# Two pairs of heads transposed as f32 products with the identity, and two constants of the scheduling planner

## The chip, the cores and the metric

One core of a Trainium2 chip. The metric is the device time of one execution in microseconds (us); lower is better. TensorE (PE) multiplies, PEld is its weight load, VectorE (DVE) and ScalarE (ACT) move results out of PSUM, GpSimd (POOL) issues most transfers.

## The reference, cut to what matters

```python
# q, k, v: (8 batches, 12 heads, 448 rows, 64), f32
scores = q @ k.transpose(...) / sqrt(64)
attn   = maximum(scores, 0)**2 / 448
x      = (attn @ v)                       # to (3584 tokens, 768)
xn     = x / rms(x) * rms_g
out    = (silu(xn @ w_gate) * (xn @ w_val)) @ w_out     # d_ff 1536
```

Heads are worked in six pairs per batch. Scores need K and q with the head dimension on the partitions, so both are transposed first. In batch 0 TensorE does that, as soon as they land.

## The kernel before

All instructions are laid down in a fixed order by a planner that runs while the program is built. It keeps an estimated time for each engine and picks the next instruction by it; on the chip each engine then simply follows its list. Where TensorE has nothing to do before the first feed-forward product, the planner inserts **fillers**: products of constants into a spare bank (psB in the profile), which keep the clock up (the run at threshold 400 shows what happens with too few). The parts that the change touches:

```python
GAP = 110.0                # ns: a smaller planned gap gets no filler
SEM, PSUM, HAND, SW = 50.0, 210.0, 200.0, 95.0    # SW: change of array mode
FLOOR = 5850.0, 8500.0, ...    # ns: the earliest planned landing of each early load
F32_T = 0
...
    if self.warm() and (not times or min(times) > t + self.GAP):
        return t, self.filler
...
def filler(self):
    s = max(self.t) + (self.SW if self.mode != "full" else 0.0)
    cost = self.fill() or 96.0           # 128x224, one product
...
# transposes(): one pair, K in 7 pieces and half of q in 2, for 2 heads
ps = bank.take("psT", BF16, [P, 1024])
for nm, j, c, w, o in steps:
    for hh in range(2):
        nc.tensor.transpose(out=ps[...], in_=ld[nm, b][...], identity=ident[:w, :w])
...
pl.task(2, {"dve": dve_cost(width, 0.52), "act": act_cost(width)}, copy, ...)   # to qkT
```

Of the kernel before, what the change touches and what calls it, by code (L numbers as in the profile page):

```python
# [9 lines left out]
BF16 = mybir.dt.bfloat16  # L10
# [4 lines left out]
U = 7  # L15
UH = 4
# [11 lines left out]
def latest(toks, at=0.0):  # L28
    for k in toks:
        if k.t is None:  # L30
            return None
        at = max(at, k.t)
    return at
# [21 lines left out]
class Planner:  # L55
# [2 lines left out]

    SEM, PSUM, HAND, SW = 50.0, 210.0, 200.0, 95.0
    WARM = 6500.0  # L60
    GAP = 110.0
    either = ("square", "squared")
    SLACK = 0.0
    PEN = 200.0
# [197 lines left out]
    def choose(self, t):  # L262
# [21 lines left out]
        for a in self.auxes + self.sneaks:  # L284
            r = a.ready()
            if r is not None:
                times.append(r)
        if self.warm() and (not times or min(times) > t + self.GAP):
            return t, self.filler
# [51 lines left out]
def kernel(  # L341
# [11 lines left out]
    nc = tc.nc  # L353
    P = nc.NUM_PARTITIONS
    B, H, S, D = q.shape
    T, DM = out.shape
    _, F = moe_w_gate.shape
    assert (T, DM) == (B * S, H * D) and 2 * D == P and S % NCH == 0 and B % 2 == 0 and S == U * D
    PC = S // NCH
# [17 lines left out]
    JOIN = 300.0  # L377
    LAG = 2800.0
    LAG0 = 2050.0
    FLOOR = 5850.0, 8500.0, 9350.0, 10450.0, 11150.0, 11850.0, 13150.0, 14900.0  # L380
    floors = []
    LASTW = (384, 192, 192)
    A2, A3, A5 = (384, 384), (256, 256, 256), (512, 256)
# [2 lines left out]
    WO = (A2, A2, A2, A2)  # L386
    ORDER = "w0-2 w2-4 k w4-6 w6-8 w8-10 K w10-12 v"
    FIRST = "k4-8 q8-12 k8-12 v0-4 v4-12 Q"
    F32_T = 0
    AGATE = 6  # L390
    THIRD = 0
    THIRDV = 3
# [24 lines left out]
    pl = Planner(nc, tc, banks, wide, None)  # L417

    def act_cost(n, per=0.8333):
        return 172.0 + per * n  # L420

    def dve_cost(n, per=1.0417):
        return 156.0 + per * n
# [9 lines left out]
    ident = const.tile([P, P], BF16, name="ident", tag="ident")  # L433
# [8 lines left out]
    ld, ldtok, ldhome = {}, {}, {}  # L442
# [3 lines left out]
    def issue(fn, nbytes, run, need=(), rate=None, ahead=8):  # L446
# [8 lines left out]
        def go(e):  # L455
# [4 lines left out]
            lag = LAG0 if dma["t"] < 5000.0 else 1900.0 if dma["t"] < 6500.0 else LAG  # L460
            at = max(dma["t"] + lag, FLOOR[len(floors)] if len(floors) < len(FLOOR) else 0.0)
            floors.append(at)
# [132 lines left out]
    qkT, kTok, qTok = {}, {}, {}  # L595

    def new_qkT(b):
        if b not in qkT:
            qkT[b] = qtpool.tile([P, HP, 2, S], BF16, name="qkT", tag="qkT")
        return qkT[b]  # L600

    def bank_ready():
        f = [x.free for x in banks if x.free is not None]
        return min(f) if f else None

    def wide_ready(n):
        f = sorted(x.free for x in wide if x.free is not None)
        return f[n - 1] if len(f) >= n else None

    def take_bank():  # L610
        return min((x for x in banks if x.free is not None), key=lambda x: x.free)

    def take_wide():
        return min((x for x in wide if x.free is not None), key=lambda x: x.free)

    def free_bank(bank):
        def then(end):
            bank.free = end + 60.0
        return then

    def transposes(b, pairs, c0, c1, with_k, gate=lambda: True):

        done = Tok()
        for j in pairs:
            if with_k:
                kTok[b, j] = done
            for c in range(c0, c1):
                qTok[b, j, c] = done
        toks = [identTok]
        for j in pairs:  # L630
            for nm in ("k", "q") if with_k else ("q",):
                for hh in range(2):
                    lst = ldtok[nm, b][2 * j + hh]
                    if nm == "q" and b == 0:
                        lst = [lst[0]] if c0 == 0 else [lst[-1]]
                    toks += lst
        n = (c1 - c0) * PC
        width = (S if with_k else 0) + n * len(pairs)

        def ready():  # L640
            if not gate():
                return None
            r, f = latest(toks), bank_ready()
            return None if r is None or f is None else max(r, f)

        def run(s):
            bank = take_bank()
            ps = bank.take("psT", BF16, [P, 1024])
            t = new_qkT(b)
            steps = []  # L650
            end = s
            if with_k and b == 0:
                steps += [("k", pairs[0], u, D, u % UH * P + u // UH * D) for u in range(U)]
                end += pl.SW + U * (29.2 - 56.0)
            elif with_k:
                steps += [("k", pairs[0], c, P, c * P) for c in range(UH)]
            at = S if with_k else 0
            for i, j in enumerate(pairs):
                steps += [("q", j, c, PC, at + i * n + (c - c0) * PC) for c in range(c0, c1)]
            for nm, j, c, w, o in steps:  # L660
                for hh in range(2):
                    nc.tensor.transpose(  # L662
                        out=ps[hh * D : (hh + 1) * D, o : o + w],
                        in_=ld[nm, b][:w, 2 * j + hh, c * D : (c + 1) * D],
                        identity=ident[:w, :w],
                    )
            end += 56.0 * len(steps)

            def copy(e):
                if with_k:  # L670
                    dst = t[:, pairs[0]].rearrange("p t s -> p (t s)")[:, c0 * PC : c0 * PC + width]
                    src = ps[:, :width]
                else:
                    dst = t[:, pairs[0] : pairs[-1] + 1, 1, c0 * PC : c1 * PC]
                    src = ps[:, :width].rearrange("p (j s) -> p j s", s=n)
                if e == "dve":
                    copied[b, pairs[-1]] = nc.vector.tensor_copy(out=dst, in_=src)  # L677
                else:
                    copied[b, pairs[-1]] = nc.scalar.copy(out=dst, in_=src)

            pl.task(
                2, {"dve": dve_cost(width, 0.52), "act": act_cost(width)}, copy, [Tok(end + 200.0)],
                done, free_bank(bank),
            )
            return end

        pl.auxes.append(Aux("transposes", "col", ready, run))

    def transposes_f32(j):

        done = [Tok(), Tok()]
        kTok[0, j] = done[0]
        for c in range(2):
            qTok[0, j, c] = done[1]
        toks = [identTok]
        for hh in range(2):
            toks += ldtok["k", 0][2 * j + hh] + ldtok["q", 0][2 * j + hh][:1]

        def ready():
            r, f = latest(toks), wide_ready(1)  # L700
            return None if r is None or f is None else max(r, f)

        def run(s):
            bank = take_wide()
            ps = bank.take("psT")
            t = new_qkT(0)
            parts = (
                ("k", [(u, D, u % UH * P + u // UH * D) for u in range(U)], S),
                ("q", [(c, PC, c * PC) for c in range(2)], 2 * PC),
            )  # L710
            left = [2]

            def over(t):
                left[0] -= 1
                if not left[0]:
                    bank.free = t + 60.0

            for i, (nm, steps, width) in enumerate(parts):
                for c, w, o in steps:
                    for hh in range(2):  # L720
                        nc.tensor.matmul(
                            out=ps[hh * D : (hh + 1) * D, i, o : o + w],
                            lhsT=ld[nm, 0][:w, 2 * j + hh, c * D : (c + 1) * D],
                            rhs=ident[:w, :w],
                            start=True,
                            stop=True,
                        )
                s += 2.0 * sum(w / 2.4 + 2.5 for _, w, _ in steps)

                def copy(e, i=i, width=width):  # L730
                    (nc.vector.tensor_copy if e == "dve" else nc.scalar.copy)(
                        out=t[:, j, i, :width], in_=ps[:, i, :width]
                    )

                pl.task(
                    2, {"dve": dve_cost(width), "act": act_cost(width)}, copy,
                    [Tok(s + 200.0)], done[i], over,
                )
            return s + pl.SW

        pl.auxes.append(Aux("transposes", "col", ready, run))

    def transposes_wide(b, ja, gate):
# [666 lines left out]
    identTok = pl.task(-1, {"pool": 550.0}, make_ident)  # L1410
# [27 lines left out]
        return sub.total - sum(1 for u in pl.units if u.sub is sub)  # L1438

    for j in range(HP):  # L1440
        if j < F32_T:
            transposes_f32(j)
        else:
            transposes(0, [j], 0, 2, True)
    pl.task(0, {"sp": 500.0}, load_g, [kTok[0, HP - 1]])
    for j in range(0, HP, 3):
        transposes(0, [j, j + 1, j + 2], 2, 4, False, gate=lambda: begun(a0) >= AGATE)
    for j in range(0, HP, 1 + WIDE_T):
        def gate(j=j):
            return getattr(a1, "visited", 0) >= GATE if j < 2 else begun(subs[2]) >= 3 * j - LEAD  # L1450
# [136 lines left out]
```

## Time and profile before

| | before |
|---|---|
| median of the six runs beside the changed kernel | 436.48 us (436.30 to 436.73) |
| span of the profiled run | 434.8 us |
| TensorE busy | 429.8 us |
| fillers | 78, of which 27 before the first transpose |
| first transpose | 6.39 us |
| first feed-forward product (psg) | 25.23 us |

Read it thus: from 25.23 us to the end TensorE has a dense list of feed-forward products, so its end should move with that first psg, and what the change gains or loses should show as a shift of psg. I therefore measure each run by two distances, **from the first transpose to psg** and from psg to the end of the span.

### The profile page before, as it was taken

What the parts mean: (1) busy time and instruction counts of PE and PEld (TensorE: products, weight loads), DVE (VectorE), ACT (ScalarE), POOL (GpSimd) and SP (SyncE); (2) the same over time, 40 slices, a digit from 0 to 9 for tenths busy, and PEclk for the clock granted to TensorE, in tenths of its full rate; (3) what the DMA queues carried; (4) which work ended last, traced back from release to release, by engine and by line L of the source; (5) the groups of instructions that cost most, each with busy time, mean ns of one, the idle gap of its engine ahead of it and who ended that gap; (6) DMA issues with size and microseconds to landing.
All of it is one profiled execution on the core that took longest, in us unless ns stands there. A gap on an engine that the chain in (4) does not pass through costs nothing.

```text
span 434.8 us, 12552 instructions
## 1 busy us (share of the span) xinstructions
PE 429.8 (99%) x5576; PEld 314.9 (72%) x5576; DVE 265.1 (61%) x437; ACT 251.5 (58%) x356; POOL 78.5 (18%) x97
## 2 busy tenths in 40 slices
PE   8999999999999999999999999999999999999996
PEld 6678788964579755885579855795569955699996
DVE  3898984478754676657854578567754577442200
ACT  4878873576663675757743676576744567342222
POOL 8444411062160070006200340001000000000000
PEclk9999999999999999999999999999999999999998
DMA  9999999699799599179917991166103200020023
GB/s 151 193 196 196 203 192 120 132 173 123 106 157 205 110 138 64 38 136 107 124 38 155 152 161 9 37 115 99 28 17 95 74 2 2 2 74 2 2 74 109
DMA packets 134805, 44.68 MB, mean 103 GB/s; under 512 B 104096, under 2 KB 131296, under 8 KB 134752
## 3 DMA queue, kind: packets, MB, share of 16 engines
q0 software_dynamic: 94448, 24.16, 57.7%
q1 hardware_dynamic: 39808, 19.50, 22.2%
q8 instruction: 43, 0.70, 0.7%
q10 hardware_dynamic: 496, 0.24, 0.2%
q14 instruction: 10, 0.08, 0.1%
HBM read 48.76 MB, written 11.01 MB: 137 GB/s over the span
## 4 chain that ended last, share of the span: by engine, by line
PE 98%; DMA 1%; issue 0%; DVE 0%; ACT 0%; POOLq 0%
PE psO L147 26%; PE psv L147 26%; PE psg L147 26%; PE psAV L1024 9%; PE psS L917 7%; PE psT L662 2%; PE psB L1532 1%; DMA k<-in_k_dram 1%; PE psR L938 1%; PE psSS L1206 0%; PE psSS L1130 0%; DVE qkT L677 0%; ACT ost L1336 0%; POOLq L1571 0%
## 5 line engine op out<-in xcount | busy, mean ns | idle before, releaser
L147 PE MATMUL psv<-xn,wv_sb 64*128 64x448 bf16 (+1 forms) x1296 | 170.4, 329 | 0.0
L147 PE MATMUL psg<-xn,wg_sb 64*128 64x448 bf16 (+1 forms) x1296 | 170.0, 329 | 0.0
L860 ACT ACTIVATE r<-psS 128x896 bf16<-128x896 f32 x133 | 119.1, 919 | 33.4 <-PE psS L917 32.6
L147 PE MATMUL psO<-wo_sb,hT 64*128 64x384 bf16 (+2 forms) x1464 | 132.3, 310 | 0.0
L147 PEld LDWEIGHTS <-hT 64*128 64x128 bf16 x1464 | 109.8, 94 | 14.6 <-issue 2.5
L147 PEld LDWEIGHTS <-wg_sb 64*128 64x128 bf16 x1296 | 94.9, 94 | 30.5 <-issue 3.2
L147 PEld LDWEIGHTS <-wv_sb 64*128 64x128 bf16 x1296 | 93.9, 94 | 31.4 <-issue 2.5
L866 DVE TENSOR_TENSOR r<-r 128x896 bf16<-128x896 bf16 (+1 forms) x171 | 99.9, 610 | 12.1 <-ACT r L860 11.4
L1258 DVE TENSOR_TENSOR hT<-sil,psv 128x448 bf16<-128x448 bf16 x96 | 59.2, 617 | 61.4 <-PE psv L147 61.1
L1242 ACT ACTIVATE sil<-psg 128x448 bf16<-128x448 f32 x96 | 52.3, 545 | 47.8 <-PE psg L147 47.6
L917 PE MATMUL psS<-qkT 64*128 64x448 bf16 (+1 forms) x324 | 53.0, 329 | 0.1
L1336 ACT COPY ost<-psO 128x384 f32<-128x384 f32 (+2 forms) x51 | 23.1, 453 | 50.1 <-PE psO L147 49.9
L508 POOL DMA_DIRECT2D vb<-in_v_dram x18 | 13.2, 743 | 180.8 <-PE psg L147 75.2
L1024 PE MATMUL psAV<-r,vb 64*64 64x448 bf16 (+1 forms) x756 | 43.1, 335 | 0.4
L860 ACT ACTIVATE r<-psR 128x896 bf16<-128x896 f32 (+1 forms) x24 | 20.2, 840 | 28.7 <-PE psR L938 28.7
L1055 DVE TENSOR_SCALAR xT<-psAV 128x896 bf16<-128x896 f32 (+1 forms) x20 | 20.4, 1022 | 25.8 <-PE psAV L1024 25.7
L1180 DVE SCALAR_TENSOR_TENSOR xn<-xT,g_sb,rstd 128x448 bf16<-128x448 bf16 (+1 forms) x54 | 30.2, 626 | 7.8 <-ACT rstd L1164 7.7
L555 POOL DMA_DIRECT2D kb<-in_k_dram x42 | 31.6, 795 | 13.1 <-DMA vb<-in_v_dram 5.4
L1024 PEld LDWEIGHTS <-vb 64*64 64x64 bf16 x756 | 18.5, 105 | 20.6 <-PE psAV L1024 8.5
L917 PEld LDWEIGHTS <-qkT 64*128 64x128 bf16 x324 | 19.2, 94 | 9.8 <-issue 1.1
L858 DVE TENSOR_SCALAR r<-psS 128x896 bf16<-128x896 f32 x11 | 12.0, 1087 | 17.6 <-PE psS L917 17.4
L1080 DVE TENSOR_TENSOR x2f<-xT 128x896 f32<-128x896 bf16 x19 | 20.6, 1084 | 2.0 <-ACT xT L1053 2.0
(49 smaller groups left out, 175.2 us busy)
## 6 DMA issues: line engine op xcount, KB each, us to landing
vb<-in_v_dram POOLq DMA_DIRECT2D x14, 384.0 KB, 6.5
kb<-in_k_dram POOLq DMA_DIRECT2D x42, 96.0 KB, 7.6
qb<-in_q_dram POOLq DMA_DIRECT2D x6, 672.0 KB, 10.3
out_dram<-ost SPq DMA_DIRECT2D x7, 336.0 KB, 2.8
wg_sb<-in_moe_w_gate_dram POOLq DMA_DIRECT2D x6, 384.0 KB, 13.1
wv_sb<-in_moe_w_val_dram POOLq DMA_DIRECT2D x6, 384.0 KB, 13.2
wo_sb<-in_moe_w_out_dram POOLq DMA_DIRECT2D x2, 1152.0 KB, 18.8
out_dram<-ost SPq DMA_DIRECT2D x8, 288.0 KB, 2.8
```

The source lines that it names most:

```text
L147: mm = self.nc.tensor.matmul(out=seg.bank["tile"][:, off : off + seg.w], lhsT=lhsT[prt], rhs=rhs[prt], start=(seg.first and h == 0 and i = ...
L555: lambda o=o, i=i: nc.gpsimd.dma_start(out=o, in_=i),
L860: nc.scalar.activation(out=r[:, :, :w], in_=ps[:, :, :w], func=ACT.Relu)
L866: nc.vector.tensor_tensor(out=r[:, :, :w], in0=r[:, :, :w], in1=r[:, :, :w], op=ALU.mult)
L917: nc.tensor.matmul(out=ps[:, hh, o : o + n], lhsT=t[prt, j, 0, c * P : (c + 1) * P], rhs=t[prt, j, 1, sub.q0 : sub.q0 + n], start=True, st ...
L1024: mm = nc.tensor.matmul(out=ps[hh * D : (hh + 1) * D, jj, :n], lhsT=vt[prt, 2 * (ja + jj) + hh, u * D : (u + 1) * D], rhs=r[prt, hh, o : o ...
L1055: nc.vector.tensor_scalar_mul(out=xT[at], in0=ps[:, :, :n], scalar1=inv_attn)
L1080: nc.vector.tensor_tensor(out=got["x2"][:], in0=xT[at], in1=xT[at], op=ALU.mult)
L1180: nc.vector.scalar_tensor_tensor(out=xn[:, kt, q0 : q0 + n], in0=xTs[b, 0][:, kt, q0 : q0 + n], scalar=g_sb[:, kt : kt + 1], in1=rstd[:, q ...
L1242: nc.scalar.activation(out=s[:, :m], in_=ps[:, :m], func=ACT.Silu)
L1258: nc.vector.tensor_tensor(out=h[:, fbs[0] : fbs[-1] + 1, o : o + n], in0=s[:, :m].rearrange("p (f s) -> p f s", s=n), in1=ps[:, :m].rearra ...
L1336: nc.scalar.copy(out=ost[:, c0 : c0 + w], in_=ps[:, :w])
```

## The change

Its intent: transpose the first two pairs with real products, K and q side by side across the border of two f32 banks, so that one instruction copies both; and tune the filler threshold and the first landing to that.

```diff
-    GAP = 110.0
+    GAP = 160.0
-    FLOOR = 5850.0, 8500.0, ...
+    FLOOR = 6000.0, 8500.0, ...
-    F32_T = 0
+    F32_T = 2
...
-            bank = take_bank()
-            ps = bank.take("psT", BF16, [P, 1024])
+            if f32:
+                bank = take_wide()
+                ps = bank.take("psT")[:].rearrange("p a b -> p (a b)")[:, 512 - S :]
+            else:
+                bank = take_bank()
+                ps = bank.take("psT", BF16, [P, 1024])
...
+                    if f32:
+                        nc.tensor.matmul(out=to, lhsT=rows, rhs=ident[:w, :w], start=True, stop=True)
+                    else:
+                        nc.tensor.transpose(out=to, in_=rows, identity=ident[:w, :w])
...
-                2, {"dve": dve_cost(width, 0.52), "act": act_cost(width)}, copy, ...
+                2, {"dve": dve_cost(width, 1.0417 if f32 else 0.52), "act": act_cost(width)}, copy, ...
... (an unused older variant, transposes_f32, is removed)
-            transposes(0, [j], 0, 2, True)
+            transposes(0, [j], 0, 2, True, f32=j < F32_T)
```

More of the change, by code (lines that the diff above doesn't have):

```diff
@@ L379 @@
     LAG0 = 2050.0
-    FLOOR = 5850.0, 8500.0, 9350.0, 10450.0, 11150.0, 11850.0, 13150.0, 14900.0
+    FLOOR = 6000.0, 8500.0, 9350.0, 10450.0, 11150.0, 11850.0, 13150.0, 14900.0
     floors = []
@@ L619, in free_bank, with transposes @@
         return then
-    def transposes(b, pairs, c0, c1, with_k, gate=lambda: True):
+    def transposes(b, pairs, c0, c1, with_k, gate=lambda: True, f32=False):
         done = Tok()
@@ L642, in ready @@
                 return None
-            r, f = latest(toks), bank_ready()
+            r, f = latest(toks), wide_ready(1) if f32 else bank_ready()
             return None if r is None or f is None else max(r, f)
         def run(s):
-            bank = take_bank()
-            ps = bank.take("psT", BF16, [P, 1024])
+            if f32:
[4 more added lines that the diff above has]
+                ps = bank.take("psT", BF16, [P, 1024])
             t = new_qkT(b)
@@ L661, in run @@
                 for hh in range(2):
-                    nc.tensor.transpose(
-                        out=ps[hh * D : (hh + 1) * D, o : o + w],
-                        in_=ld[nm, b][:w, 2 * j + hh, c * D : (c + 1) * D],
-                        identity=ident[:w, :w],
-                    )
+                    to = ps[hh * D : (hh + 1) * D, o : o + w]
+                    rows = ld[nm, b][:w, 2 * j + hh, c * D : (c + 1) * D]
+                    if f32:
+                        nc.tensor.matmul(out=to, lhsT=rows, rhs=ident[:w, :w], start=True, stop=True)
+                    else:
+                        nc.tensor.transpose(out=to, in_=rows, identity=ident[:w, :w])
             end += 56.0 * len(steps)
@@ L681, in run @@
             pl.task(
-                2, {"dve": dve_cost(width, 0.52), "act": act_cost(width)}, copy, [Tok(end + 200.0)],
+                2, {"dve": dve_cost(width, 1.0417 if f32 else 0.52), "act": act_cost(width)}, copy, [Tok(end + 200.0)],
                 done, free_bank(bank),
@@ L685, in run @@
             return end
-        pl.auxes.append(Aux("transposes", "col", ready, run))
-    def transposes_f32(j):
-        done = [Tok(), Tok()]
-        kTok[0, j] = done[0]
-        for c in range(2):
-            qTok[0, j, c] = done[1]
-        toks = [identTok]
-        for hh in range(2):
-            toks += ldtok["k", 0][2 * j + hh] + ldtok["q", 0][2 * j + hh][:1]
-        def ready():
-            r, f = latest(toks), wide_ready(1)
-            return None if r is None or f is None else max(r, f)
-        def run(s):
-            bank = take_wide()
-            ps = bank.take("psT")
-            t = new_qkT(0)
-            parts = (
-                ("k", [(u, D, u % UH * P + u // UH * D) for u in range(U)], S),
-                ("q", [(c, PC, c * PC) for c in range(2)], 2 * PC),
-            )
-            left = [2]
-            def over(t):
-                left[0] -= 1
-                if not left[0]:
-                    bank.free = t + 60.0
-            for i, (nm, steps, width) in enumerate(parts):
-                for c, w, o in steps:
-                    for hh in range(2):
-                        nc.tensor.matmul(
-                            out=ps[hh * D : (hh + 1) * D, i, o : o + w],
-                            lhsT=ld[nm, 0][:w, 2 * j + hh, c * D : (c + 1) * D],
-                            rhs=ident[:w, :w],
-                            start=True,
-                            stop=True,
-                        )
-                s += 2.0 * sum(w / 2.4 + 2.5 for _, w, _ in steps)
-                def copy(e, i=i, width=width):
-                    (nc.vector.tensor_copy if e == "dve" else nc.scalar.copy)(
-                        out=t[:, j, i, :width], in_=ps[:, i, :width]
-                    )
-                pl.task(
-                    2, {"dve": dve_cost(width), "act": act_cost(width)}, copy,
-                    [Tok(s + 200.0)], done[i], over,
-                )
-            return s + pl.SW
         pl.auxes.append(Aux("transposes", "col", ready, run))
@@ L1440 @@
     for j in range(HP):
-        if j < F32_T:
-            transposes_f32(j)
-        else:
-            transposes(0, [j], 0, 2, True)
+        transposes(0, [j], 0, 2, True, f32=j < F32_T)
     pl.task(0, {"sp": 500.0}, load_g, [kTok[0, HP - 1]])
```

## The prediction

> **What bounds the kernel now.** I read the page first, then twenty-microsecond stretches of each engine, then the order in time and the chain of waits of the first 26 us, then the groups of those 26 us by shape.
>
> The page says that one engine sets the time. These are its busy times and the lines of the chain that ended last:
>
> ```profile
> PE 429.8 (99%) x5576; PEld 314.9 (72%) x5576; DVE 265.1 (61%) x437; ACT 251.5 (58%) x356; POOL 78.5 (18%) x97
> ...
> PE psO L147 26%; PE psv L147 26%; PE psg L147 26%; PE psAV L1024 9%; PE psS L917 7%; PE psT L662 2%; PE psB L1532 1%; DMA k<-in_k_dram 1%; PE psR L938 1%; PE psSS L1206 0%; PE psSS L1130 0%; DVE qkT L677 0%; ACT ost L1336 0%; POOLq L1571 0%
> ```
>
> TensorE is the bound, and the feed-forward products alone are 78% of the chain. The stretches show where its few idle microseconds lie (columns: stretch, length, then busy time and count of PE, PEld, DVE, ACT, POOL, then clock and DMA):
>
> ```profile
> 0.00:20.00 20.00, 18.57 (x316) 12.75 (x316) 11.66 (x25) 12.57 (x17) 13.67 (x24) 1.00 1.27 170
> 20.00:40.00 20.00, 20.00 (x365) 15.32 (x360) 16.96 (x33) 15.22 (x22) 9.05 (x12) 1.00 1.46 197
> ```
>
> 1.43 us are idle in the first 20; after that 0.26 us in four dips until 420 us, and 3.3 us in the tail. But busy is not useful: the first 26 us hold 78 matmuls on psB, 12.1 us, whose result nobody reads. They keep the clock up while attention of batch 0 waits for data and for the copies. The first feed-forward matmul starts at 25.23 us, and behind it TensorE never stops. So whatever moves that first psg moves the end by the same amount, and the change, which touches only the start of batch 0, can be worth no more than it gains or loses before 25.23 us.
>
> The order in time around the changed transposes (start, length, engine, line, what; the idle time before and its releaser in brackets):
>
> ```profile
> 6.39 0.41 PE L662 MATMUL psT<-ident,k 64*64 64x64 bf16 x14 [0.41 <-DMA k<-in_k_dram]
> 6.73 0.14 PEld L662 LDWEIGHTS <-qb 112*64 112x64 bf16 x4
> 6.73 0.29 PE L662 MATMUL psT<-ident,qb 112*64 112x112 bf16 x4
> ...
> 7.06 0.51 DVE L677 COPY qkT<-psT 128x672 bf16<-128x672 bf16 x1 [5.54 <-PE psT L662]
> ...
> 7.50 0.11 PEld L1532 LDWEIGHTS <-const-bfloat16-1.0 128*128 128x128 bf16 x2
> 7.51 0.37 PE L1532 MATMUL psB<-const-bfloat16-1.0 128*128 128x224 bf16 x2
> 7.62 0.72 ACT L679 COPY qkT<-psT 128x672 bf16<-128x672 bf16 x1 [3.52 <-PE psT L662]
> 7.80 0.11 PEld L917 LDWEIGHTS <-qkT 64*128 64x128 bf16 x4 [0.19 <-DVE qkT L677]
> ```
>
> The first K arrives at 6.35 us. Two pairs are transposed in 0.56 us each (6.39 to 6.95, 6.95 to 7.50); DVE copies pair 0, ACT pair 1; the first scores wait for DVE's copy. That copy is on the path to the first scores, but not plainly on the path to 25.23 us: the next pairs are transposed at 9.15 us, after the next K transfer, whose landing a queue of the pool engine saw at 8.94 us. From there on ACT and DVE, with the rectified scores, are the nearer limit (ACT 3.83 and DVE 4.11 of the 4.5 us from 8.5 to 13).
>
> **What the Trainium skill says.** "VectorE: DVE Perf Modes", section "Why PSUM operands drop a tier", caps a PSUM source at two elements a cycle, and at one for fp32. The trace agrees on the first: 672 bf16 columns in 504 ns. On the second it has only other operations, below. "TensorE: Matmul & The Clock Gate", Part 4, says that a transpose "doesn't count as PE-busy the same way" for the clock gate; that would be a reason for real products. The trace shows no harm to mend: psB matmuls last 391 ns while cold, up to about 5.5 us, but the median of all 78 is 263 ns and those right behind the transposes run at the short length. "Perfetto Trace Analysis", section "Transposes", asks for the transpose operation rather than a product. No product with the identity is in this trace to compare. "PSUM — Partial Sum Buffer", the four PSUM rules, says that one matmul's output fits one bank; the change obeys it by placing K's 448 columns at the end of one bank and q's 224 at the start of the next, so that one copy can read both.
>
> **The change, part by part.** For pairs 0 and 1 of batch 0, 36 transposes into one bf16 bank each become 36 products with the same identity into two f32 banks.
>
> TensorE: the same 18 stationary loads and 18 moving streams per pair, of the same columns. K's go at 24 ns each (0.34 us for 14), q's four take 0.22. I expect 0.56 us per pair again: 0.
>
> DVE, pair 0: the closest f32 rows in the first 26 us are
>
> ```profile
> L677 DVE COPY qkT<-psT 128x672 bf16<-128x672 bf16 x6 | 2.9, 504 | 5.7 <-PE psT L662 5.5
> L858 DVE TENSOR_SCALAR r<-psS 128x896 bf16<-128x896 f32 x2 | 2.2, 1087 | 0.1
> ...
> L858 DVE TENSOR_SCALAR r<-psR 128x448 bf16<-128x448 f32 x1 | 0.6, 624 | 0.9 <-PE psR L938 0.9
> ```
>
> From 448 to 896 columns it gains 463 ns, so 672 columns from f32 take 624 + 232 = 856 ns, 352 ns more than now (mean times stand after the bar and comma). Which engine takes the copy is decided by the kernel's own planner when the program is built: it takes the earlier start, and DVE in a tie, so the longer DVE cost should not move pair 0 to ACT.
>
> ACT, pair 1: 544 ns for 448 f32 columns, 918 for 896, hence 731 for 672 against 719 now: +12 ns.
>
> So unit 0, the first scores, starts about **0.35 us later**, near 8.15 us. What of it goes further? The residual scores psR and unit 1 need pair 1 as well, whose ACT copy ends at 8.34 us in either kernel; psR should stay within 0.1 us of 8.43. Only the rectification of unit 0 slips, from 8.23 to about 8.55. ACT then runs two of them, 1.75 us, until about 10.3, and its next job starts at 10.38 now: the 0.4 us that ACT is idle there takes up the slip. DVE can square the residual in place of unit 0. I leave 0 to 0.15 us at the first psg.
>
> Planner constants: the first landing is planned at 6000 ns instead of 5850. By the planner's own sums the fillers before it stay 27 (700 + 95 + 27 x 189 = 5898, past 5850 but short of 6000), so TensorE's real start stays at 6.39, tied to the transfer. Behind it the plan runs 0.1 us later, closer to the chip. A filler will go only into a planned gap of over 160 ns, not 110. One filler with its change of mode costs 95 + 96 = 191 ns in the plan, so in a gap of 110 to 160 it overran by 31 to 81 ns. Single fillers stand at 8.95, 12.98 and 20.75 us; I can't know without building how many had so small a gap. If one to three vanish, 0.03 to 0.25 us come back, where the data was there.
>
> In their place the longer wait for pair 0 takes more fillers: 6000 + 95 + 411 + 200 + 856 + 50 = 7612 ns planned for the first scores, 7159 before, so about five fillers where two stood. They lie in the wait and cost nothing.
>
> Sum: +0.35 at unit 0, of which 0 to +0.15 survives; -0.03 to -0.25 from fillers; -0.1 to +0.1 from a plan that falls out differently. Centre **-0.15 us**.
>
> **Rivals.** First: DVE becomes the bound of the start. DVE is busy 2.00 of 2.00 us from 10 to 12 and 1.88 in the next two, so a slip that does not fit the gap at 9.3 would travel to the end whole. For it: that saturation. Against it: five of the first eight microseconds DVE idles, and the order of squares can change. It would make 436.7 us.
>
> Second: the copy was never the limit and the landing of K is. Nothing before 8.94 us matters, pairs 2 to 5 go where they went, and the time is 436.3. The idle 0.4 us of ACT speaks for it.
>
> Third: products keep the clock up better than transposes, and a start that is sometimes cold is mended. Three runs within 0.3 us and warm fillers at 7.5 us speak against. It would bring up to 1 us, my estimate from cold and warm filler spacing over some five microseconds with real work; I give it little.
>
> Fourth: the static order reshuffles later (bank rotation, units of batch 1). TensorE being full from 25 us on, only the start and the four small dips, 0.26 us, can react: 0.3 us either way.
>
> **Range and chances.** The surviving pieces add to roughly -0.5 to +0.4 us about 436.3, plus 0.15 us of scatter as in the three runs. So **436.1 us**, range 435.4 to 437.0. Two per cent is 8.7 us; the whole part touched holds only 12.1 us of filler, and no step here comes near taking or adding 8.7. Faster 0.01, same 0.98, slower 0.01.
>
> **What would show it.** Right: DVE's pair-0 copy near 856 ns, ACT's near 731, transposition still 0.56 us per pair, unit 0 near 8.15 us, psR near 8.43, ACT's gap near 10 us shrunk, fewer single fillers, first psg at 25.0 to 25.3 us and the same distance from there to the end. Wrong: products that run slower or faster than 24 ns each; the copy given to ACT; a psR that waits for a wide bank, since two of three now hold transposes; or a first psg that moved by more than 0.5 us, which would say that the start hung on unit 0 or on fillers more than I think.

## The result, and the profile after

The changed kernel took **435.93 us** (median of six, 435.62 to 436.35) against 436.48 (436.30 to 436.73). The ratio is 0.9987, 95% interval 0.9974 to 1.0: the same within 2%, and about half a microsecond faster. (A ratio is the mean time of one kernel's fast runs over that of the other's in the same rounds, so not quite the ratio of the medians.)

The page of the changed kernel, its line of busy times, and the first two stretches (columns as before):

```profile
PE 428.4 (99%) x5573; PEld 314.1 (72%) x5573; DVE 264.7 (61%) x437; ACT 252.0 (58%) x356; POOL 78.3 (18%) x97
```

```profile
0.00:20.00 20.00, 18.05 (x327) 12.46 (x327) 12.35 (x27) 12.83 (x18) 14.09 (x24) 1.00 1.27 168
20.00:40.00 20.00, 19.91 (x374) 15.74 (x372) 17.73 (x34) 15.54 (x22) 8.55 (x12) 1.00 1.46 197
```

Three fillers less. The 1.4 us less of busy TensorE are mostly not theirs: the 27 opening fillers took 4.11 us here and 5.20 in the profile of before, because they came up to speed earlier, and a second profile of the changed kernel has 429.7 us. First three more lines of the order in time before, then that of the changed kernel, in answer to the lines of the prediction:

```profile
7.81 0.36 PE L917 MATMUL psS<-qkT 64*128 64x224 bf16 x4
...
8.43 0.29 PE L938 MATMUL psR<-qkT 64*64 64x224 bf16 x4
...
25.23 0.27 PE L147 MATMUL psg<-xn,wg_sb 64*128 64x224 bf16 x1
```

```profile
5.99 0.41 PE L670 MATMUL psT<-ident,k 64*64 64x64 bf16 x14 [1.10 <-DMA k<-in_k_dram]
...
6.66 0.86 DVE L683 CAST qkT<-psT 128x672 bf16<-128x672 f32 x1 [5.14 <-PE psT L670]
...
7.11 0.66 PE L1481 MATMUL psB<-const-bfloat16-1.0 128*128 128x224 bf16 x5
7.22 0.72 ACT L685 CAST qkT<-psT 128x672 bf16<-128x672 f32 x1 [3.12 <-PE psT L670]
...
7.71 0.37 PE L869 MATMUL psS<-qkT 64*128 64x224 bf16 x4
8.00 0.29 PE L890 MATMUL psR<-qkT 64*64 64x224 bf16 x4
...
24.16 0.27 PE L147 MATMUL psg<-xn,wg_sb 64*128 64x224 bf16 x1
```

K landed 0.40 us earlier here than in the profile of before (first transpose 5.99 against 6.39), so times must be compared from the first transpose. The first scores come after 1.72 us instead of 1.42 (+0.30), psR after 2.01 instead of 2.04, psg after 18.17 instead of 18.84 (-0.67). From psg to the end of the span it is 409.84 us instead of 409.57 (+0.27). So the spans differ by -0.40 - 0.67 + 0.27 = -0.80 us (434.0 against 434.8), and only the last two terms, together -0.40, are the change's, if the landing is chance.

### The profile page after: what moved, and what is told of

It reads as the page before. It is cut to its first block, busy times and chain, and to the rows that moved or that the text cites. A ratio compares the mean times of both kernels' runs of the same rounds, so it can differ in the third digit from the quotient of the medians.

```text
span 434.0 us, 12544 instructions
## 1 busy us (share of the span) xinstructions
PE 428.4 (99%) x5573; PEld 314.1 (72%) x5573; DVE 264.7 (61%) x437; ACT 252.0 (58%) x356; POOL 78.3 (18%) x97
## 4 chain that ended last, share of the span: by engine, by line
PE 98%; DMA 1%; issue 0%; ACT 0%; DVE 0%; POOLq 0%
PE psO L147 26%; PE psv L147 26%; PE psg L147 26%; PE psAV L976 9%; PE psS L869 7%; PE psT L672 1%; PE psB L1481 1%; DMA k<-in_k_dram 1%; PE psR L890 1%; PE psSS L1082 0%; PE psT L670 0%; PE psSS L1158 0%; ACT xT L1005 0%; DVE x L1018 0%; ACT ost L1288 0%
## 5 line engine op out<-in xcount | busy, mean ns | idle before, releaser
L1032 DVE TENSOR_TENSOR x2f<-xT 128x896 f32<-128x896 bf16 x18 | 19.5, 1085 | 2.0 <-ACT xT L1005 2.0
```

The costliest lines, as they stand in the source:

```text
L1032: nc.vector.tensor_tensor(out=got["x2"][:], in0=xT[at], in1=xT[at], op=ALU.mult)
```

## The experiments

Twelve runs were made, in three sets of four, each set on one chip beside the kernel before. A warning on the runs first. Most runs of a kernel lie within about 1 us, but some runs of most kernels, before too, took 439 to 444 us, and only the longest of them count as slow by the rule used for the ratios (over 1.5% above the kernel's fastest). The ratios of the sets thus carry most of them along and are blurred. **I call runs over 438.5 us "long" and give, beside the number of long ones, the median of the others.** Each of the 29 long runs has a mean granted clock of 0.982 to 0.988; every other run for which the record gives a clock has 0.997 to 1.000. What a long run looks like, the set at threshold 200 shows.

| kernel | others: median (number) | long | before, same set: median (number), long | first transpose to psg |
|---|---|---|---|---|
| changed, as predicted on | 435.93 (6) | 0 | 436.48 (6), 0 | 18.17 us |
| changed again | 436.15 (2) | 4 | 436.33 (9), 4 | 18.41 |
| threshold alone | 435.89 (5) | 1 | same set | 18.03 |
| both constants, no f32 | 436.59 (5) | 0 | same set | 19.47 |
| f32, no constants | 437.29 (5) | 0 | same set | 20.81 |
| changed order, bf16 | 436.20 (5) | 1 | 436.60 (10), 1 | 18.17 |
| threshold 400 | none | 6 | same set | 20.83 (a long run) |
| f32 and threshold | 437.36 (5) | 0 | same set | 20.14 |
| before again | 436.70 (1) | 0 | same set | 18.84 |
| changed, third time | 436.28 (5) | 1 | 436.47 (7), 4 | 18.29 |
| threshold alone, again | 435.74 (5) | 1 | same set | 18.09 |
| threshold 200 | 435.76 (3) | 3 | same set | 21.47 (a long run) |
| short fillers | 437.11 (3) | 3 | same set | 18.91 |

**The theories.** A: the gain comes from what stands in TensorE's list, above all fillers, not from the f32 step. B: the products, or their one copy, gain. C: the earlier landing of K in the changed kernel's profile is chance.

### The changed kernel again, and the kernel before again

No edit.

> The changed kernel once more, to see how much of the two profiles' difference belongs to the change. In the first pair of profiles K of the first pairs landed at 5.95 us (changed) and 6.35 us (before), and the warm clock came earlier. If this is chance (theory C), the landing here falls anywhere from 5.9 to 6.4 us and only the distance from the start of the first transpose to the first psg stays: 18.2 us against 18.8 us before. If the change moved the landing, it is 5.95 again. Time 435.7 to 436.2 us, 0.3 to 0.7 below before.

> The kernel before once more, for its profile alone. If the landing of K and the moment of the warm clock are chance, the first transpose falls somewhere from 5.9 to 6.4 us, not at 6.39 again by rule, and the distance from it to the first psg stays near 18.8 us (18.0 with the threshold at 160).

C holds. The first transpose began at 6.00 us in the changed kernel, with K already there, and at 6.47 in the kernel before; over all profiles it ranges from 5.92 to 6.47, without regard to the kernel. The moment at which psB goes from 391 to about 260 ns moves too: 27 fillers ended at 4.89 us in one run of the changed kernel and at 5.98 in the next, where the first transposes still ran at half speed (0.51 us for K's 14 in place of 0.34), so its 18.41 us hold about 0.2 of that. The clock column says 1.00 throughout, but only because the trace holds no clock record before the warming: its first record, of full clock, begins at 3.55 us in the first profile of the changed kernel and at 6.69 in the second. Until then the durations alone tell. The kernel before repeated its 18.84 us exactly. Of six runs of the changed kernel four were long, which I had not expected at all.

### The threshold alone

```diff
-    GAP = 110.0
+    GAP = 160.0        # on the kernel before
```

> The kernel before with only the filler threshold at 160 instead of 110. The build's plan is the same as before but for five fillers less (73 against 78), the planned first psg is the same. Theory A (the gain comes from where fillers and other work stand in TensorE's order): fillers that overran their gap delay real work, so 0.1 to 0.4 us faster than before, and the single fillers at 8.95, 12.98 and 20.75 us mostly gone. Theory B (the f32 products or their copy are what gains): same as before within 0.1 us.

It gains as much as the whole change: 435.89 us against 436.33. The plan is that of before, but for five fillers (and, following from those, the interleaving of the two array halves within a few score units). An example, in the order in time of the kernel before and then of this one:

```profile
12.69 0.37 PE L917 MATMUL psS<-qkT 64*128 64x224 bf16 x4
12.99 0.27 PE L1532 MATMUL psB<-const-bfloat16-1.0 128*128 128x224 bf16 x1
13.31 0.37 PE L917 MATMUL psS<-qkT 64*128 64x224 bf16 x4
```

```profile
12.31 0.56 PE L917 MATMUL psS<-qkT 64*128 64x224 bf16 x8
12.80 0.86 PE L1532 MATMUL psB<-const-bfloat16-1.0 128*128 128x224 bf16 x7
```

Before, the second score unit began 0.62 us after the first, with one filler and a change of mode each way between; now the two run as one block of eight, and that filler stands behind them, where six became seven. DVE's copies do not explain it: before, the second unit waited for a copy that had ended at 12.75 us and began at 13.31; now the same copy ends at 12.37 and the unit begins at 12.51, while DVE's next copy runs until 12.93. From the first transpose to the first psAV it is 7.40 us instead of 7.95, to psg 18.03 instead of 18.84: 0.81 us for five fillers of 0.1 us each. But my expectation had the wrong fillers in mind: the single one at 8.95 stayed (8.70 in this run); the groups at 7.51, 10.76 and 15.96 lost one each, and the one at 20.75 and the four at 21.85 became one group of three. Some 0.2 us of the 0.81 is lost again near 99 us, where the second group of psAV of batch 2 starts 0.40 us after its psR instead of 0.23. (The threshold alone on its second chip lost nothing there.)

### Both constants, without f32

```diff
-    F32_T = 2
+    F32_T = 0          # on the changed kernel
```

> The changed kernel with no pair as an f32 product: both constants changed, transposes in bf16. Theory B: back to the time of before, 436.5. Theory A: the time follows the order the planner happens to make, not the f32 step; its plan holds 82 fillers, against 75 in the changed one and 78 in before, and puts the first psg 0.8 us later than the changed one's; I expect 436.3 to 437.2 us, slower than the changed kernel.

436.59 us, and 19.47 us to psg. The shifted floor takes back what the threshold gave, because the order comes out otherwise: 82 fillers.

### The f32 step without the constants, and with the threshold

```diff
-    GAP = 160.0
-    FLOOR = 6000.0, 8500.0, ...
+    GAP = 110.0        # on the changed kernel; only in the first of the two
+    FLOOR = 5850.0, 8500.0, ...
```

> The changed kernel with the old constants (threshold 110, first floor 5850): f32 products alone. Theory B: the gain stays, 435.9 us. Theory A: without the constants the plan holds 92 fillers and puts the first psg 1.4 us later than the changed kernel's, of which 0.9 is won back after it; I expect 436.3 to 437.3 us, no faster than before.

> The changed kernel with the old first floor 5850 but the new threshold 160. Its plan is that of the f32 products with both old constants but for 6 fillers less. Theory A: 0.2 to 0.5 us better than that kernel's 437.3, so 436.8 to 437.1 us, and still slower than before: the f32 step asks for the shifted floor to land on a good order. Rival (threshold alone is worth 0.5 us on any order and floors do not matter): 435.9 us, as the changed kernel.

Both fall behind before, by 0.96 and 0.76 us on their chips: 437.29 and 437.36 us. So B is refuted as a general gain (the first of the two has no such standstill as is shown below). Nor did the threshold help here as I expected: psg came 0.67 us nearer (20.14 against 20.81), but psg to the end grew from 408.6 to 409.3 us, and the time stayed. That loss stands at one place, the first psR of batch 1; here it is without the threshold, then with it:

```profile
35.89 0.36 PE L890 MATMUL psR<-qkT 64*64 64x448 bf16 x4
```

```profile
34.94 0.35 PE L890 MATMUL psR<-qkT 64*64 64x448 bf16 x1
35.71 0.38 PE L890 MATMUL psR<-qkT 64*64 64x448 bf16 x3 [0.43 <-issue]
```

Between the first and the second product of psR TensorE stood still, with no wait that the profile shows; from psg to that place, and from there to the end, the two runs keep step within 0.06 us. Why it stood still, and whether it did in all five runs (437.14 to 437.52 us), is open. The other effect is plain work: without the constants psg comes 1.97 us later than in before, but the rest is 1 us shorter, as 36 products more of the attention (28 psAV, 4 psS, 4 psR) stand in front of psg. So a gain at psg need not reach the end. With f32 and the threshold, floor 6000 in place of 5850 is worth 1.1 to 1.4 us (435.93 to 436.28 against 437.36, on other chips), some 0.75 of them this standstill; without f32 it costs 0.7 (436.59 against 435.89).

### The changed order, with bf16 transposes

The planner still reckons with f32 and two banks; only what is emitted changes.

```diff
-                ps = bank.take("psT")[:].rearrange("p a b -> p (a b)")[:, 512 - S :]
+                ps = bank.take("psT", BF16, [P, 2, 1024])[:].rearrange("p a b -> p (a b)")
-                    if f32:
-                        nc.tensor.matmul(out=to, lhsT=rows, rhs=ident[:w, :w], start=True, stop=True)
-                    else:
-                        nc.tensor.transpose(out=to, in_=rows, identity=ident[:w, :w])
+                    nc.tensor.transpose(out=to, in_=rows, identity=ident[:w, :w])
```

> The changed kernel's order kept instruction for instruction (the planner still reckons with an f32 copy of 856 ns and two banks), but the 36 instructions of pairs 0 and 1 are bf16 transposes again, and DVE copies in about 504 ns. Theory A (only the order and the fillers matter): the five fillers behind the transposes hold TensorE until the f32 copy would be done anyway, so unit 0 starts at most 0.1 us earlier and the time is that of the changed kernel, 435.7 to 436.1 us. Theory B (the products themselves gain): back to 436.4 or more.

The order in time of this kernel:

```profile
6.08 0.41 PE L669 MATMUL psT<-ident,k 64*64 64x64 bf16 x14 [0.88 <-DMA k<-in_k_dram]
...
6.75 0.51 DVE L680 COPY qkT<-psT 128x672 bf16<-128x672 bf16 x1 [5.22 <-PE psT L669]
...
7.19 0.66 PE L1478 MATMUL psB<-const-bfloat16-1.0 128*128 128x224 bf16 x5
...
7.79 0.37 PE L866 MATMUL psS<-qkT 64*128 64x224 bf16 x4
```

DVE is done 0.35 us sooner, yet the scores begin 1.71 us after the first transpose, where they began with f32 (1.72): the five fillers hold the list until then. psg follows after 18.17 us, the same to the hundredth. The time, 436.20 us, is 0.4 below before on its chip; the changed kernel was 0.2 to 0.55 below on its chips. **In this order, products and transposes are worth the same**; what is left between them is under the scatter, and the two ran on different chips.

### Thresholds of 400 and 200

```diff
-    GAP = 110.0
+    GAP = 400.0        # on the kernel before; 200.0 in the other
```

> The kernel before with the filler threshold at 400: the same plan again, 53 fillers in all instead of 78 (73 at 160). Theory A: each short filler taken from in front of useful work gains a little more: 435.3 to 435.9 us, better than both kernels. Rival (fillers are needed for the clock, or for the order to hold): the clock drops in the first 25 us, matmuls of 391 ns appear between 7 and 25 us, and the time rises to 437 or more.

> Threshold 200 on the kernel before: 70 fillers, nearly the same plan. If fewer fillers go on helping, 435.5 to 435.9 us; if the clock starts to suffer as it did at 400 (53 fillers), the profile shows matmuls at half clock between 8 and 19 us or more of the runs are slow: 437 us or a mix.

The rival won at 400: 438.70 to 441.55 us. The stretches show why (the last three columns are clock, DMA share and GB/s):

```profile
6.00:8.00 2.00, 1.68 (x41) 1.09 (x41) 0.99 (x2) 0.51 (x1) 2.00 (x3) 1.00 1.33 162
8.00:10.00 2.00, 1.82 (x32) 1.02 (x33) 1.71 (x4) 1.91 (x3) 1.08 (x2) 0.60 1.35 174
10.00:12.00 2.00, 1.94 (x29) 1.14 (x29) 1.64 (x4) 1.23 (x3) 1.90 (x4) 0.50 1.45 194
```

The granted clock falls to 0.50 at 8.38 us and is back at 1.00 at 18.62: the 53 fillers are too few. At 200 the runs split into 435.72, 435.76 and 436.28 us and 439.27, 440.22 and 441.12 us, and the profiled one was the run of 439.27:

```profile
7.00:7.50 0.50, 0.50 (x16) 0.28 (x9) 0.37 (x1) 0.08 (x1) 0.50 (x2) 1.00 1.49 168
7.50:8.00 0.50, 0.50 (x6) 0.20 (x5) 0.31 (x1) 0.50 (x1) 0.50 (x1) 0.64 1.54 188
8.00:8.50 0.50, 0.50 (x5) 0.16 (x5) 0.50 (x1) 0.50 (x2) 0.27 (x1) 0.50 1.38 196
```

So one long run is shown to be an opening at half clock, from 7.64 to 17.88 us (the stretch from 16 to 18 us has a mean clock of 0.53, the next 1.00), which put psg at 27.67. Both falls, here and at 400, came 3.41 us after the trace's first record of full clock (4.22 and 4.97 us) and lasted 10.24 us. What decides is not shown. It is not the idle time of TensorE in those 3.41 us alone: 1.09 and 1.14 us in the two runs that fell, but 1.10 (changed) and 1.18 (threshold alone, again) in two that kept the clock.

The long runs of the other kernels had a lower mean clock too; that theirs fell in the opening is likely, not shown, as no long run was profiled but at 200 and 400. Nor does the number of fillers explain how often it happens. The three kernels with 82 to 92 fillers had no long run in 15, and those with 73 to 78 had 9 in 41 (before), 5 in 18 (changed), 2 in 12 (threshold alone) and 1 in 6 (changed order, bf16). But before itself went from 1 in 11 to 4 in 11 from set to set, and the 148 short fillers below, about as much filler time as in before, had 3 in 6.

### The changed kernel against the threshold alone, on one chip

No edit to the changed kernel; the threshold alone as above.

> The changed kernel a third time, beside the next run on the same chip. 435.6 to 436.2 us in its usual runs, 0.2 to 0.6 below before; some runs 4 us or more longer, as 4 of 6 in the second set, are expected again and are left out of the comparison.

> The kernel before with only the threshold at 160, on the same chip as the changed kernel. Theory A: the threshold alone holds the whole gain, so the two medians of usual runs agree within 0.15 us. Rival (f32 and floor add to it): the changed kernel is 0.3 us or more ahead.

The simpler kernel is not behind: 435.74 us (435.56 to 435.98 but for the long one) against 436.28 (435.67 to 437.01). Neither expectation came true: the medians lie further apart than 0.15 us, and the other way round from the rival. How far it leads is not safe: 0.54 us here, 0.26 on the chip where both ran first, with only two usual runs of the changed kernel to compare. The slowest usual run of the changed kernel, 437.01 us, is the profiled one, and its trace shows 0.7 us that have nothing to do with the opening: TensorE waits for v of batch 2. First the same place in the first profile of the changed kernel:

```profile
97.84 0.95 PE L976 MATMUL psAV<-r,vb 64*64 64x448 bf16 x16
```

```profile
98.34 0.38 PE L976 MATMUL psAV<-r,vb 64*64 64x448 bf16 x2
99.06 0.94 PE L976 MATMUL psAV<-r,vb 64*64 64x448 bf16 x14 [0.34 <-DMA vb<-in_v_dram]
```

So the scatter of usual runs has a source behind psg as well.

Over all usual runs the means are 435.91 (10 runs, threshold alone), 436.08 (13, changed) and 436.52 (32, before). With one constant changed, the threshold alone does at least as well as the changed kernel and better than before, and has long runs like them.

### Short fillers

```diff
-            bank.fill = ps[:, 0, :HALF] if bank in wide else ps[:, :HALF]      # HALF = 224
+            bank.fill = ps[:, 0, :112] if bank in wide else ps[:, :112]
... (the second operand is cut alike, and a default cost in the planner)
-        cost = 96.0 if max(pl.t) > pl.WARM else 189.0
+        cost = 49.0 if max(pl.t) > pl.WARM else 94.5
```

> The kernel before, threshold 110, with fillers of 112 columns instead of 224: half as long (49 ns planned), 148 of them, so an overrun of a gap is at most half as long while TensorE stays as busy. Theory A: overrun is what costs, so about as good as the threshold at 160 or better, 435.6 to 436.1 us, with the clock safe. Rival (the number of fillers costs, through instruction issue): 436.5 us or more.

A miss: 437.11 us in three runs, three long ones, and 18.91 us to psg, where before has 18.84. So halving the longest overrun gained nothing at psg. With 148 fillers every wait is filled more finely, and a change of mode is still paid for each gap. Whether that or the number of instructions costs, I can't tell from this run. Most of what the profiled run (436.70 us) loses on before from psg on, about 0.37 of 0.45 us, arises near 98 us again, where 16 psAV take 1.33 us in place of 0.95.

## Why the prediction was right, and where its terms were not

The total was right: 436.1 us, measured 435.93, in the range, and "same". Luck had a part in it: the terms add up to -0.15 us, the medians differ by 0.55, and the centre came near only because the wrong terms were small against the range or cancelled. Its steps fared unevenly. One of its own signs of being wrong appeared: psg moved by more than 0.5 us (by 1.07, of which 0.67 are not the landing), which was to say that the start hung on unit 0 or on fillers more than thought. The runs speak for the fillers and the order, not for unit 0.

- **Pair by pair the hardware steps held.** Products take 0.56 us per pair (5.99 to 6.55, 6.55 to 7.11). DVE's copy of 672 f32 columns took 859 ns (predicted 856; 505 for bf16), ACT's 719 (731; 719 for bf16). DVE kept pair 0. Exactly five fillers stood behind. The first scores slipped by 0.30 us (0.35), psR by nothing.
- **"0 to 0.15 us at the first psg": 0.** The same order with the short copy has the same 18.17 us.
- **"-0.03 to -0.25 from fillers" was mis-sized.** The threshold alone brought psg 0.75 to 0.81 us nearer and the time down by 0.44 to 0.73 us, on the plan of before. I had counted the overrun of single fillers past a planned gap; but a removed filler gives back its whole stay and its changes of mode where the data was there (shown above for one of the five), and groups lost fillers as well as singles.
- **"-0.1 to +0.1 from a plan that falls out differently" was mis-sized most**, as was the fourth rival's 0.3 us either way. The f32 step on the old floor costs about 1.5 us against the threshold alone (437.36 against 435.74 to 435.89, other chips), half of it the standstill at 35 us, whose cause is open; the shifted floor gives most of it back, and without f32 the floor costs 0.7. These two large terms cancel, and so the total looked like the sum of small ones.
- **"Whatever moves that first psg moves the end by the same amount" failed.** The changed kernel gained 0.67 us at psg and lost 0.27 behind it, with the same work (fillers apart) in front of psg; why, no run shows. F32 without the constants lost 1.97 and won 1 us back, as work moved in front of psg. And there are waits behind psg, at 35 and 98 us.
- **The first rival, DVE as the bound,** did not happen: DVE's slip vanished. **The second** was right that the copy is not the limit, wrong that the next pairs go where they went: they began 2.53 us after the first transpose instead of 2.76.
- **The third rival, the clock, I had dismissed on three close runs.** Half-clock openings exist, and are the largest effect, 3 us and more. But the f32 products did not mend them: 5 long runs in 18 against 9 in 41 before.

## What to carry to other kernels

Measure a new instruction in the old order and the new order with the old instruction before crediting either: here the order did all that can be told from the scatter, and the instruction nothing. In a statically ordered list a filler is not free because its engine is idle in the plan; it delays whatever was ready. But take too many away and the clock falls, in some runs only, so count the long runs and do not look at the median alone. And follow a gain to the end of the span: a later wait can eat it.

## What the Trainium skill lacked or had wrong

- "TensorE: Matmul & The Clock Gate", "Why this matters for your kernels", asks for no idle gap of TensorE over about 3 us to keep the clock. It was not enough here: in the long run at threshold 200 the longest gap before the fall was 1.09 us (ended at 6.20 us), TensorE was then busy without a break, and the clock fell to 0.50 at about 7.7 us. The run of the threshold alone on the same chip had a gap of 1.18 us (ended at 6.23) and kept 1.00. The page speaks of short idle times between groups as well, but gives no length for them; the runs give no sharp one either.
- The same page, Part 4, says that transposes do not count as busy for the clock in the same way. No run here shows a benefit of products: the long runs are 5 of 18 with products (changed) and 1 of 6 with transposes in the same order; before has 9 of 41.
- "Perfetto Trace Analysis", "Transposes", prefers the transpose to a product. For 64- and 112-column pieces both took 0.56 us per pair; the trace shows no difference on TensorE.
